# One core, two attentions: KH of group 0 in two equal loads, row maxima from tile 12, Q of the next unit asked for in the 9th step

## The chip, the core and the metric

The kernel runs on one core of a Trainium2 chip. The metric is the device time of one execution in microseconds; below 0.3% (some 2.8 us) two versions of this kernel cannot be told apart.

## The reference

Input x has 2048 rows of 448. Two attentions with 16 heads of 28 read it, and a gate per row mixes their outputs:

```python
g = sigmoid((x * gate_w).sum(-1, keepdims=True))
a = A_ref(x, A_wqkv, A_wo)   # each position attends to 8 positions back, 2 apart
b = B_ref(x, B_wqkv, B_wo)   # softmax(q k^T * Dh**-0.5) v over all 2048 positions
return g * a + (1 - g) * b
```

All is float32. A product of two float32 matrices is made of three products of "high" and "low" parts (a value rounded to fp32r, and the rest).

## The kernel before, in words

**Tile stage.** 92 tiles (`tiles`, indices 0 to 91; the loop at L451) project x. Tiles 0 to 27 give Q and K of B, 128 features by 512 positions each; tiles 28 to 43 give V of B; tiles 44 to 91 give q, k and v of A. The first 12 tiles are (position block, feature block) pairs from `tiles`: K of head group 0 comes from tiles 0, 3, 6 and 7, one block of 512 positions each. Tiles 0 to 9 (`FULL` = 10) use the whole TensorE array and four accumulators of two banks (`PS`) in turn. From tile 10 on the array is used in two halves of 64 rows (`project_halves`, L310): each half sums half of the products in its own bank of `PJ` = PS0 or PS1, and ScalarE copies both out (L348, L362). A Q or K tile has 21 such half matmuls.

**Row maxima (S1).** The softmax of B needs the row maxima before the scores. They come from a first score matrix that uses the high parts only. In 80 of the tiles, from `S1_START` on, four half-array score matmuls (`s1_half`, L155; L144) stand between the products, two into each pair of banks of `PM` = PS2 and PS3, and VectorE reduces each pair (L162). In the tile with index `S1_START` the two pairs stand later in the tile than in the others (L318). The first of these four tiles reads columns 0 to 511 of `KH[0]`, the next one columns 512 to 1023, and so on. The rest of the maxima are made in the main loop, three score matmuls a step (L1014, L148).

**SP's order.** All loads and stores of this stage go out on one queue, SP, in program order: for each of the tiles 0 to 9 two stores (`qk_store`, L331) of its high and low parts to DRAM, and between them the loads of weights, of Q for the maxima (`load_qhi`, L131) and of `KH[0]` back from DRAM (`load_k`, L104: four DMAs, one per head, of 28 rows each). A DMA that must wait holds back all that are behind it on SP.

**Main loop.** 16 units (head group, block of 512 queries) of 16 steps, `st` = 0 to 255 (L1052). A step multiplies 128 keys with the unit's Q (L1024), ScalarE takes the exponentials (L1027, two of 128 x 1024), TensorE sums them with V (L978), and VectorE reduces maxima. Work is hung on steps by hand ("pre" at the step's start, "dve", "end"). GpSimd (POOL) runs the local attention A, 8 chunks of 56 columns, in an order that a planner with fixed costs writes out, and between these pieces the parts of B's ending that are listed next. `load_q(u + 1)` (L119) asks for Q of the next unit: four DMAs of high parts, four of low parts, two of the negated maxima (10 in all), at the start of step 12 of unit u.

**Ending of a unit (L907 to L920).** During the unit that follows, counted in its steps: 1 copy the sums out (`osb`); 3 store the row sums; 6 VectorE inverts them, POOL multiplies them with the gate (`finv`, L847), SP stores the result (`rs<-finv`, L851); 8 SP loads it back, spread over partitions (`rbc`, four DMAs, L856); 12 POOL multiplies (`on`, L885); 15 ScalarE rounds the product (`onhi`, L889, ahead of that step's exponentials); then `onlo` on POOL and the stores. Loads of the low parts of K (`KL<-qk_lo`) for later groups hang on the end of steps 30, 72 and 136, and SP's loads of A's chunks (`qt`, `kt`, `vt`) go out at the start of a step, behind its "pre" work.

Of the kernel before, what the change touches and what calls it, by code (L numbers as in the profile page):

```python
# [15 lines left out]
S, D, H, DH = 2048, 448, 16, 28  # L16
# [4 lines left out]
NU = NG * NB  # L21
# [4 lines left out]
def gated_mix_kernel(ctx: ExitStack, tc: tile.TileContext, xT, xn, gw, wA, wB, woAB, out):  # L26
# [4 lines left out]
    qk_hi = dram.tile([2 * D, S], F32R, name="qk_hi")  # L31
# [41 lines left out]
    KH = [cp.tile([128, S], F32R, name=f"KH{i}") for i in range(2)]  # L73
# [26 lines left out]
    def dma_r(dst, src):  # L100
        nc.sync.dma_start(dst.bitcast(F32), src.bitcast(F32))  # L101


    def load_k(g, t, src, c=slice(0, S)):  # L104
        for h in range(4):
            r = D + 112 * g + DH * h
            dma_r(t[32 * h:32 * h + DH, c], src[r:r + DH, c])
# [98 lines left out]
    with tc.tile_pool(name="xp", bufs=1) as xp, tc.tile_pool(name="wp", bufs=2) as wp:  # L206
# [28 lines left out]
        def split_x(nb):  # L235
            r, t = xst[:, nb, 0:3, :], xst[:, nb, 3, :]
            for kt in range(3):
                split(xh[nb][:, kt, :], xl[nb][:, kt, :], r[:, kt, :])
            tail = xh[nb][:, 3, :]
            nc.scalar.activation(tail, t, AF.Copy)  # L240
            o = LOW[nb]
            nc.vector.tensor_tensor(out=tail[o], in0=t[o], in1=tail[o].bitcast(F32), op=ALU.subtract)
# [3 lines left out]
        def load_w(wi, tails=(False, True)):  # L246
            src, cols = WSRC[wi]
            if wi not in wraw:
                wraw[wi] = raw3(), wp.tile([128, 450], F32, tag="wt", name="wt"), sum(c1 - c0 for c0, c1 in cols) + 2 * (wi == GATE)
            r, t, _ = wraw[wi]  # L250
            for tail in tails:
                o = 0
                for c0, c1 in cols:
                    e = o + c1 - c0
                    if tail:
                        both(t[:, o:e], src[384:448, c0:c1])
                    else:
                        nc.sync.dma_start(r[:, :, o:e], src[0:384, c0:c1].rearrange("(k p) c -> p k c", p=128))
                    o = e

                if wi == GATE:
                    if tail:
                        both(t[:, o:o + 2], gw[0:2, 384:448].rearrange("i p -> p i"))
                    else:
                        for kt in range(3):
                            nc.sync.dma_start(r[:, kt, o:o + 2],
                                              gw[0:2, 128 * kt:128 * kt + 128].rearrange("i p -> p i"))

        def split_w(wi, kts):
            if wi not in wsets:  # L270
                wsets[wi] = [wp.tile([128, 4, 450], F32R, tag=g, name=f"{g}{wi}") for g in ("wh", "wl")]
            wh, wl = wsets[wi]
            r, t, n = wraw[wi]
            for kt in kts:
                split(wh[:, kt, :n], wl[:, kt, :n], r[:, kt, :n] if kt < 3 else t[:, :n], nc.gpsimd)
# [151 lines left out]
        def split_third():  # L427
            c = slice(256, 384)
            for kt in range(3):
                split(wh0[:, kt, c], wl0[:, kt, c], wr1[:, kt, 128:256])  # L430
            split(wh0[:, 3, c], wl0[:, 3, c], wt0[:, c])
# [9 lines left out]
        tiles.extend((4 + i, "a", i, j) for i in range(3) for j in js)  # L441


        FULL, S1_START = 10, 11

        parts = []

# [3 lines left out]
        for n, t in enumerate(tiles):  # L451
            wi = t[0]
            for w in loads:
                if loads[w] == n:
                    load_w(w)
            for w in splits:
                i, k = (n - splits[w][0]) * splits[w][1], splits[w][1]
                if 0 <= i < 4:
                    split_w(w, range(i, i + k))
            if n == 0:  # L460
                split_third()
            if n in (3, 5):
                split_x((n + 1) // 2)
            if n < FULL:
                project(n)
            else:
                project_halves(n, [S1_START <= m < S1_START + 80 for m in (n, n + 1)])
            if t[1] == "qk":
                qk_tile(n, t[2], t[3])
            elif t[1] == "v":  # L470
                add_halves(n, V[:, t[2], :, 0:DH])
            else:
                a_tile(n, t[2], t[3])
            if n == 0:
                split_x(1)
            while fini and fini[0][0] <= n:
                fini.pop(0)[1]()
            if n in (2, 3):
                load_w(1, (n == 3,))
            if n == 3:  # L480
                load_qhi(0)
            if n == 7:
                load_k(0, KH[0], qk_hi, slice(0, 1536))
            if n == 8:
                load_k(0, KH[0], qk_hi, slice(1536, S))
            if n == 16:
                for i in (1, 2):
                    nc.sync.dma_start(a_scr[i][:, 0:NJ, :].rearrange("c j e -> c (j e)").rearrange(
                        "c (a b) -> c a b", b=NJ), omg[0:8, None, :].to_broadcast([8, 56, NJ]))
            if n == 32:  # L490
                nc.gpsimd.memset(V[:, :, :, DH:], 1.0)
            if n == 22:
                load_k(1, KH[1], qk_hi)
            if n == 62:
                load_k(0, KL[0], qk_lo)
            if parts and parts[0][0] <= n:
                _, u, t = parts.pop(0)
                max_store(u, max_turn(t.bitcast(F32)))
            if finished and n < len(tiles) - 3:
                u = finished.pop(0)  # L500
                parts.append((n + 3, u, max_parts(u)))
            if n == 64:
                gate = []
                for sgn, dst in ((-1.0, g_t), (1.0, omg)):
                    e = sp.tile([128, NJ], F32, name="ez")
                    nc.scalar.activation(e, zt, AF.Exp, scale=sgn)
                    nc.gpsimd.tensor_tensor(out=e, in0=e, in1=V[:, 0, :, DH], op=ALU.add)
                    gate.append((dst, e))
            if n in (66, 68):
                nc.vector.reciprocal(*gate.pop(0))  # L510
            if n == 70:
                r = max_turn(omw)
                for a in range(4):
                    nc.sync.dma_start(og_scr.rearrange("(j p) -> j p", j=NJ)[:, 32 * a:32 * a + 32],
                                      r[32 * a:32 * a + NJ, :])
            if n == 76:
                load_q(0)
# [170 lines left out]
    for c in range(8):  # L688
# [20 lines left out]
        n = 0  # L709
# [342 lines left out]
    for u in range(NU):  # L1052
        g, b = divmod(u, NB)
        for kt in range(NJ):
            st = NJ * u + kt
            now[0] = st
            if kt == 12 and u + 1 < NU:
                load_q(u + 1)
            run("pre", st)
            issue("sp", st, 0)  # L1060
            if st >= A_START:
                issue("pool", st, 4.2)
            if not adone and not any(lists.values()) and st > stored[0]:
                a_done(st)
            cur = {}
            left = s1e - s1c[0]
            for a in scores(u, kt, cur):
                if a == 2:
                    run("mid", st)
            run("dve", st)  # L1070
            if u and kt == 6:
                late["dve"] += 0.25
            if finished:
                v = finished.pop(0)
                t = max_parts(v)
                late["dve"] += 0.3
                turned = {}
                lag = 2 if v < NU - 1 else 1
                at("dve", st + lag, lambda t=t, w=turned: w.update(r=max_turn(t.bitcast(F32))))
                at("end", st + lag, lambda v=v, w=turned: max_store(v, w["r"]))  # L1080
            issue("dve", st, DLIM)
            issue("act", st, 0)
            run("act", st)
            if prev is not None:
                do_av(prev)
            prev = (kt, cur, g)
            if OPS and st >= OPS[0]:
                op_some(st, 7)
            run("end", st)
            step = 2.25 if left else 2.1  # L1090
            late["dve"] = max(0.0, late["dve"] + 0.58 * min(3, left) - step)
            late["pool"] = max(0.0, late["pool"] - step)
            if st == OP0 + 31:
                op_load_b(2, 3)
            if not OPS and s1c[0] == s1e:
                s1_close()
                at("pre", st + 1, lambda: op_t(0))
                at("end", st + 1, lambda: op_split(0))
                OPS.append(st + 2)
# [61 lines left out]
```

## Time and profile before

| | |
|---|---|
| runs | 916.68, 918.61, 918.80 us; median 918.61 |
| profiled execution | 918.6 us, of which the instructions span 916.7 us |
| busy share: PE, VectorE, ScalarE, POOL | 99%, 80%, 71%, 68% |
| mean granted TensorE clock | 0.997 of full speed |
| tile stage, main loop | to about 258 us, from there to 887 us |

PE is TensorE; an instruction counts as busy while it is in the pipeline, so 99% says only that little time passes without any. The views used below: the list of waits (who waited for whom), the instructions of an engine in order of time, the chain of waits that ended last, and busy time by stretch.

### The profile page before, as it was taken

To read this page: it belongs to the slowest core of one execution; us is meant where nothing else is said; L and a number is where in the kernel's file an instruction comes from. 1 tells how busy PE (TensorE), PEld (TensorE's weight loads), DVE (VectorE), ACT (ScalarE), POOL (GpSimd) and SP (SyncE) were. 2 spreads that over 40 slices of the span, in tenths; PEclk is the share of its full clock that TensorE was granted. 3 is DMA by queue.
4 is the path that set the end of the run, shared out by engine and by line. 5 is a ranking of instruction groups with operands and counts; after the bars stand their busy time and mean duration, and the time that the engine had idled before them with its cause. 6 is when DMAs were issued, how large, how long until landed. Compare 5 with 4: busy or idle time off the path is not lost.

```text
span 916.7 us, 20680 instructions
## 1 busy us (share of the span) xinstructions
PE 904.7 (99%) x8396; PEld 539.3 (59%) x8396; DVE 731.4 (80%) x977; ACT 652.1 (71%) x802; POOL 620.9 (68%) x485
## 2 busy tenths in 40 slices
PE   9899999999999999999999999999999999999998
PEld 7688999999954444444444444443444444466667
DVE  6388999999979999999999999999999888400012
ACT  6356434343378898888888898988989889854551
POOL 2289856564469799999999999999994952300100
PEclk9999999999999999999999999999999999999999
DMA  9867603444372341335135232530412123553422
GB/s 268 275 203 220 177 11 83 132 122 120 103 249 70 97 126 44 86 112 127 44 96 153 86 102 55 144 79 23 115 42 53 34 66 102 145 162 112 131 90 93
DMA packets 101118, 104.29 MB, mean 114 GB/s; under 512 B 61652, under 2 KB 71252, under 8 KB 100240
## 3 DMA queue, kind: packets, MB, share of 16 engines
q1 hardware_dynamic: 100880, 102.72, 39.5%
q8 instruction: 65, 1.06, 0.5%
q10 hardware_dynamic: 144, 0.26, 0.1%
q14 instruction: 29, 0.24, 0.1%
HBM read 61.99 MB, written 40.48 MB: 112 GB/s over the span
## 4 chain that ended last, share of the span: by engine, by line
PE 80%; POOL 11%; DMA 3%; SPq 2%; ACT 2%; issue 1%; DVE 0%; POOLq 0%; ACTq 0%; DVEq 0%
PE T L1024 22%; PE av L978 20%; PE r L298 15%; PE T L817 8%; PE r L293 7%; PE r L144 4%; POOL prod L613 3%; POOL oat L668 3%; PE T L144 3%; POOL prod L663 2%; SPq L101 2%; ACT P L1027 1%; PE T L795 1%; DMA KL<-qk_lo 1%; DMA V<-in_xT 1%
## 5 line engine op out<-in xcount | busy, mean ns | idle before, releaser
L1027 ACT ACTIVATE P<-T 128x1024 f32<-128x1024 f32 x512 | 497.4, 1025 | 81.0 <-PE T L1024 79.6
L148 DVE TENSOR_REDUCE MX<-T 128x1 f32<-128x512 f32 x470 | 441.3, 954 | 33.6 <-PE T L144 19.6
L978 PE MATMUL av<-P,V 128*32 128x512 f32 x2048 | 272.7, 605 | 0.0
L1024 PEld LDWEIGHTS T<-QH,KH 30*128 30x128 f32 x1024 | 90.8, 181 | 222.4 <-ACT P L1027 199.9
L144 PE MATMUL T<-KH,QP 28*128 28x512 f32 x704 | 219.6, 454 | 0.1
L162 DVE TENSOR_REDUCE MX<-r 128x2 f32<-128x1024 f32 x160 | 192.5, 1221 | 28.3 <-PE r L144 23.6
L1024 PE MATMUL T<-QH,KH 30*128 30x512 f32 x1024 | 211.2, 489 | 3.0 <-ACT P L1027 2.0
L1024 PE MATMUL T<-QH,KL 28*128 28x512 f32 x1024 | 185.7, 395 | 0.0
L1024 PE MATMUL T<-QL,KH 28*128 28x512 f32 x1024 | 183.5, 392 | 0.0
L613 POOL TENSOR_TENSOR prod<-qt,kt 128x896 f32<-128x896 f32 x64 | 135.2, 2117 | 1.4 <-DMA kt<-a_scr 1.4
L362 ACT ACTIVATE raw<-r 128x896 f32<-128x896 f32 (+1 forms) x64 | 58.9, 921 | 96.7 <-PE r L298 96.7
L668 POOL TENSOR_TENSOR oat<-oat,prod 128x896 f32<-128x896 f32 x56 | 118.3, 2113 | 2.4
L144 PE MATMUL r<-KH,QP 64*128 64x512 f32 x320 | 98.9, 393 | 3.4 <-DMA KH<-qk_hi 3.4
L144 PEld LDWEIGHTS T<-KH,QP 28*128 28x128 f32 x704 | 86.0, 181 | 27.1 <-ACT P L1027 20.3
L663 POOL TENSOR_TENSOR prod<-vt,L 128x896 f32<-128x896 f32 x56 | 95.6, 1708 | 0.5
L363 POOL TENSOR_TENSOR ast<-raw 128x448 f32<-128x448 f32 x48 | 55.5, 1156 | 57.8 <-ACT raw L362 49.4
L1024 PEld LDWEIGHTS T<-QL,KH 28*128 28x128 f32 x1024 | 93.3, 184 | 0.0
L1024 PEld LDWEIGHTS T<-QH,KL 28*128 28x128 f32 x1024 | 91.8, 183 | 0.9
L298 PE MATMUL r<-wh,xh 64*128 64x448 f32 (+1 forms) x512 | 87.8, 363 | 0.0
L978 PEld LDWEIGHTS av<-P,V 128*32 128x32 f32 x2048 | 40.3, 108 | 77.2 <-issue 72.2
L805 DVE TENSOR_TENSOR oalo<-T,oah 128x384 fp32r<-128x384 f32 x16 | 8.9, 557 | 90.8 <-ACT onhi L804 87.7
L298 PE MATMUL r<-wh,xl 64*128 64x448 f32 (+1 forms) x384 | 70.9, 363 | 0.0
(110 smaller groups left out, 1157.0 us busy)
## 6 DMA issues: line engine op xcount, KB each, us to landing
a_scr<-ast SPq DMA_DIRECT2D x24, 448.0 KB
qk_hi<-qkh SPq DMA_DIRECT2D x24, 256.0 KB
qk_lo<-qkh SPq DMA_DIRECT2D x24, 256.0 KB
rbc<-rs SPq DMA_DIRECT2D x60, 64.0 KB
QP<-qk_hi SPq DMA_DIRECT2D x64, 56.0 KB
KL<-qk_lo SPq DMA_DIRECT2D x16, 224.0 KB
QH<-qk_hi SPq DMA_DIRECT2D x64, 56.0 KB
QL<-qk_lo SPq DMA_DIRECT2D x64, 56.0 KB
```

The lines of the kernel that those rows point to most:

```text
L144: nc.tensor.matmul(bank, qhis[u][h % 2][r, 128 * qs:128 * qs + 128], KH[u // NB % 3][r, 512 * kc:512 * kc + 512], start=True, stop=True)
L148: r = nc.vector.tensor_reduce(MX[:, n % NMX:n % NMX + k], bank, axis=X, op=ALU.max)
L162: nc.vector.tensor_reduce(m, PM[k], axis=X, op=ALU.max)
L293: nc.tensor.matmul(bank, ws[c][rows, k, t[4]:t[4] + 128], x, start=first, stop=last)
L298: nc.tensor.matmul(bank[:, 0:cols], x, ws[c][rows, k, 0:cols], start=first, stop=last)
L613: nc.gpsimd.tensor_tensor(out=p, in0=qt[c], in1=kvt["k", c % 2][:, HALO - DIL * w:HALO - DIL * w + NJ, :], op=ALU.mult)
L663: nc.gpsimd.tensor_tensor(out=dst.rearrange("p j (h d) -> p j h d", d=DH), in0=kvt["v", c % 2][:, HALO - DIL * w:HALO - DIL * w + NJ, :].r ...
L668: nc.gpsimd.tensor_tensor(out=oat[c], in0=oat[c], in1=oat[c, w], op=ALU.add)
L817: writes(bank, nc.tensor.matmul(bank[:, :D], src, wo[c][:, k, :], start=(first and k == ks[0] and i == 0), stop=(last and k == ks[-1] and ...
L978: nc.tensor.matmul(av[32 * h:32 * h + 32, :], V[:, kt, 4 * g + h, :], tiles_[h], start=(kt == 0), stop=(kt == NJ - 1), skip_group_check=True)
L1024: nc.tensor.matmul(bank[a], (KH[g % 3], KH[g % 3], KL[g % 2])[t][r, ks], (qh, ql, qh)[t][r, :], start=(t == 0), stop=(t == 2))
L1027: e = nc.scalar.activation(p, RP[0] if a == "2" else mine, AF.Exp, scale=SCALE).ins
```

## The change

Three edits. `KH[0]` was loaded as columns 0 to 1535 behind tile 7's stores and 1536 to 2047 behind tile 8's; now columns 0 to 1023 go out behind tile 6's stores and 1024 to 2047 behind tile 8's. The maxima start in tile 12 and end in tile 91 (tile 11 to 90 before). `load_q(u + 1)` stands at step 8 of units 0 to 11 and stays at step 12 in the later ones.

```diff
-        FULL, S1_START = 10, 11
+        FULL, S1_START = 10, 12
...
-            if n == 7:
-                load_k(0, KH[0], qk_hi, slice(0, 1536))
-            if n == 8:
-                load_k(0, KH[0], qk_hi, slice(1536, S))
+            if n in (6, 8):
+                load_k(0, KH[0], qk_hi, slice(512 * (n - 6), 512 * (n - 6) + 1024))
...
-            if kt == 12 and u + 1 < NU:
+            if kt == (8 if u < 12 else 12) and u + 1 < NU:
                 load_q(u + 1)
```

## Rows read from the trace of the kernel before

**Rows 1.** Page, part 4: share of the chain of waits by engine.
```profile
PE 80%; POOL 11%; DMA 3%; SPq 2%; ACT 2%; issue 1%; DVE 0%; POOLq 0%; ACTq 0%; DVEq 0%
```

**Rows 2.** Waits of PE, whole span: us in total, times, longest us.
```profile
PE r L144 <- DMA KH<-qk_hi: 3.4, 2, 2.2
...
PE T L1024 <- DMA QH<-nm: 0.7, 1, 0.7
```

**Rows 3.** ScalarE in time, 30 to 76 us: start, duration, instruction, [idle before].
```profile
36.23 1.03 ACT L348 ACTIVATE raw<-r 128x1024 f32<-128x1024 f32 x1 [2.14 <-PE r L293]
44.82 1.03 ACT L348 ACTIVATE raw<-r 128x1024 f32<-128x1024 f32 x1 [7.57 <-PE r L293]
...
50.65 1.03 ACT L348 ACTIVATE raw<-r 128x1024 f32<-128x1024 f32 x1 [1.47 <-PE r L144]
```

**Rows 4.** Busy time by stretch: length, PE/PEld/DVE/ACT/POOL (count), clock, DMA share, GB/s.
```profile
41.30:44.70 3.40, 3.24 (x16) 2.80 (x18) 1.96 (x2) 0.00 (x0) 0.00 (x0) 0.50 0.83 295
```

**Rows 5.** SP in time, 0 to 50 us: tile 7's store, KH's load.
```profile
32.96 0.59 SPq L101 DMA_DIRECT2D qk_hi<-qkh  x1
...
35.79 1.60 SPq L101 DMA_DIRECT2D KH<-qk_hi  x4
```

**Rows 6.** Chain of waits, 30 to 46 us: tile 6's store, KH.
```profile
31.58 4.15 DMA qk_hi<-qkh
...
37.01 4.32 DMA KH<-qk_hi
```

**Rows 7.** PE and VectorE in time, 246 to 270 us.
```profile
255.20 0.39 PE L144 MATMUL r<-KH,QP 64*128 64x512 f32 x1
...
258.17 0.49 PE L144 MATMUL T<-KH,QP 28*128 28x512 f32 x1
...
255.63 1.22 DVE L162 TENSOR_REDUCE MX<-r 128x2 f32<-128x1024 f32 x1 [0.23 <-PE r L144]
```

**Rows 8.** SP in time, 400 to 480 us (units 4, 5).
```profile
421.97 0.34 SPq L851 DMA_DIRECT2D rs<-finv  x1
422.41 1.64 SPq L101 DMA_DIRECT2D KL<-qk_lo  x4
424.14 1.70 SPq L856 DMA_DIRECT2D rbc<-rs  x4
...
460.73 0.42 SPq L602 DMA_DIRECT2D qt<-a_scr  x1
...
462.16 1.83 SPq L856 DMA_DIRECT2D rbc<-rs  x4
```

**Rows 9.** Chain of waits, 420 to 440 us: KL's fourth head.
```profile
423.67 6.16 DMA KL<-qk_lo
```

**Rows 10.** SP in time, 560 to 625 us (units 8, 9).
```profile
570.52 1.70 SPq L856 DMA_DIRECT2D rbc<-rs  x4
...
611.61 1.69 SPq L101 DMA_DIRECT2D QH<-qk_hi  x4
...
615.05 1.07 SPq L101 DMA_DIRECT2D QH<-nm  x2
```

**Rows 11.** POOL in order of time: `on` in units 4 and 8.
```profile
432.38 1.29 POOL L885 TENSOR_TENSOR on<-osb,rbc 128x512 f32<-128x512 f32 x1
...
580.14 1.29 POOL L885 TENSOR_TENSOR on<-osb,rbc 128x512 f32<-128x512 f32 x1
```

**Rows 12.** `on` in unit 5, its own view: duration, first and last start.
```profile
L885 POOL TENSOR_TENSOR on<-osb,rbc x1: 1288/1288/1288, 472.0 to 472.0; 128x512 f32<-128x512 f32 x1
```

**Rows 13.** ScalarE in order of time: `onhi` in units 4, 5 and 9.
```profile
437.14 0.63 ACT L889 ACTIVATE onhi<-on 128x512 fp32r<-128x512 f32 x1
...
473.89 0.63 ACT L889 ACTIVATE onhi<-on 128x512 fp32r<-128x512 f32 x1
...
619.58 0.63 ACT L889 ACTIVATE onhi<-on 128x512 fp32r<-128x512 f32 x1 [1.03 <-POOL on L885]
```

**Rows 14.** Waits of POOL, 309 to 700 us: total, times, longest.
```profile
POOL nmt L181 <- ACT nmv L180: 4.1, 1, 4.1
```

## The prediction

> **What bounds the kernel now.** I read the chain of waits first. PE carries 80% of it and POOL 11% [rows 1], so TensorE sets the time except in stretches where POOL does; PE's own list of waits says where something else enters. It has few: 3.4 us for `KH` at the first maxima and 0.7 us for the last part of a unit's Q [rows 2]. The edits touch both, and the list understates the one and overstates the other.
>
> The `KH` wait costs more than 3.4 us. ScalarE copies tile 10 out at 36.23 and tile 11 at 44.82 us; the two tiles that follow take 50.65 - 44.82 = 5.83 us, so 2.91 us each [rows 3]. Tile 11 took 8.59 us, 5.7 us too long. The rest is the clock: after the idle time the granted clock stands at 0.50 (1.2 in place of 2.4 GHz) for the 3.4 us from 41.30 on [rows 4], which costs half of that, 1.7 us.
>
> The 0.7 us for Q are worth nothing by themselves if POOL is late anyway. POOL waits once between 309 and 700 us, at its start, for ScalarE [rows 14]; from there it runs without a gap. Its product `on` feeds ScalarE's `onhi`, which stands ahead of a step's exponentials, and with them ahead of PE. In unit 9 `onhi` had to wait 1.03 us for it [rows 13]. So from 309 to 619 us the path is POOL's: whatever PE gains in between it loses again at 619 us, and each microsecond that POOL waits in there comes through. After that wait the margin in unit 9 is zero; in unit 5 it is 473.89 - (472.0 + 1.29) = 0.6 us [rows 12, 13].
>
> **Edit 1 and 2: the maxima start a tile later, `KH` in halves.** A Q or K tile has 21 half matmuls and 4 more with maxima: 2.91 / 25 = 0.117 us each. Tile 11 without them takes 21 x 0.117 = 2.45 us in place of 8.59: -6.1 us. Tile 91 gets them instead: 4 x 0.117 = +0.5 us. Sum -5.6 us, if no new wait comes. That depends on two landings.
>
> First half. Its stores (tiles 0 and 3) are long out. It takes the place of tile 7's store on SP, so it is issued from 32.96 on, four DMAs in some 1.6 us [rows 5], the last at about 34.2; with the 4.32 us that `KH`'s fourth head took [rows 6] it lands at 38.5. ScalarE's copy of tile 10 at 36.23 [rows 3] follows the tile's end by some tenths; I put the end at 35.8. Tile 11 then ends at 38.3, and in tile 12 twelve half matmuls stand ahead of the first maxima: needed at 39.7. Margin 1.2 us: cost 0 (bounds 0 and, if it waits half as long as before, 2.8 us).
>
> Second half. Tile 7's store is now issued 1.6 us later, at 34.6, and with 4.15 us [rows 6] is out at 38.8. Four more issues, the last at some 40.2; with 4.32 us it lands at 44.5. Tile 14 needs it at 38.3 + 2 x 2.91 + 4 x 0.117 = 44.6. That is on the edge. I take 0; bounds 0 and 2.8 us (1.1 us late and one stretch at half clock, 1.7 us).
>
> Tile 91's maxima end against the main loop. There the second reduction ended at 255.63 + 1.22 = 256.85, 1.65 us after the last score matmul of its tile (255.20) began [rows 7]. In tile 91 some six half matmuls, 0.7 us, follow that matmul; then comes the main loop, whose third instruction group writes `T1`, which I take to lie in the bank pair that is still being reduced. It waits about 0.9 us. Before, this step had waits of its own, shorter (its first maxima began with the loop, at 258.17 [rows 7], the next two behind ScalarE's copy of tile 91). I take +0.7 us; bounds 0 and 1.2. POOL is put off with PE: it waits for ScalarE at 309 us [rows 14].
>
> **Edit 3: Q asked for at step 8.** Q's ten DMAs occupy SP from 611.61 to 616.12, 4.5 us [rows 10]. Before, they came behind `rbc`, which POOL's `on` needs; now they come ahead of it, since `rbc` hangs on the end of step 8 and the loads on its start. Ahead of them stays `rs<-finv` of step 6, which SP holds until POOL has made `finv` [rows 8]. So `rbc` lands 4.5 us later wherever SP went from one to the other without a pause. Is there room? Where `rbc` goes out soon after `rs` with nothing large ahead of it, and `on` comes four steps later, I count on it. In three units a large load stands ahead of `rbc`, and there it is short:
> - Unit 4: SP issued `rs`, `KL`, `rbc` at 421.97, 422.41 and 424.14 [rows 8]. `KL` landed at 423.67 + 6.16 = 429.83 [rows 9] and `rbc`, behind it, before `on` began without a wait at 432.38 [rows 11]; I take 431.0. With 4.5 us it lands at 435.5: POOL waits 3.1 us (by the ends of the bracket, 1.9 to 4.5).
> - Unit 5: SP's `qt` and `kt` (460.73) stand between, `rbc` follows at 462.16 [rows 8]; with 6.2 us as `KL` had, 468.4. It moves by 4.5 and by POOL's 3.1, to 476.0; `on` would come at 472.0 + 3.1 = 475.1 [rows 12]: 0.9 to 1.0 more (bounds 0 and 4.5).
> - Unit 8: `rbc` at 570.52 behind `KL` [rows 10], so landed at 576.7; moved by 4.5 + 4.1 it is there at 585.3, `on` would come at 580.14 + 4.1 = 584.2 [rows 11]: 1.1 more (bounds 0 and 4.5).
>
> POOL loses 5.2 us by unit 9; I bound it by 0 and 7. PE follows: in unit 4 `onhi` still comes in time (435.5 + 1.3 = 436.8 against 437.14 [rows 13]), in unit 5 it waits some 4 us, and in unit 9 PE is 5.2 us later than without the edit. If PE's clock falls in that long wait, the 1.7 us come out of the 5.2, since POOL goes on. The 0.7 us of [rows 2] vanish as a wait and are part of what POOL then takes back. A's chunk loads are put off by 4.5 us as well; POOL never waited for one in this stretch [rows 14], and the code asks for each at least four steps, some 9 us, ahead of its use: 0.
>
> **Sum.** The profiled execution took 918.6 us (span 916.7 and 1.9 around it), the median of the runs. 918.6 - 5.6 + 0.7 + 5.2 = 918.9 us.
>
> **A rule against the middle of this sum.** Here `rbc`'s time depends on what SP sent before it: `KL`'s 224 KB took 6.16 us in such a row [rows 9]. The Trainium skill, "DMA: Bandwidth & Descriptors", section "Anatomy of one DMA — SWDGE (gpsimd) path", puts a DMA of the other issuing path at a fixed 2.0 us plus its bytes over 436 GB/s. By that an estimate for `KL` is 2.5 us and for one `rbc` 2.2 us; `rbc` would be there before `on` in all three units, POOL would wait for nothing, and the time would be that of the first rival below. The trace does not agree: 6.16 us.
>
> **The rivals.**
> - `rbc` is in time, POOL loses under 2.5 us. For it: the landing of `rbc` has no row of its own, only brackets, and with the early ends of all three (1.9 + 0 + 0) POOL loses 1.9. With none lost: 918.6 - 5.6 + 0.7 = 913.7 us. Against it: `KL`'s landing is a row, and it moves with the 4.5 us.
> - The second half of `KH` is the new wait (slower than before). Its place is tile 14, its point of decision a landing after 44.6 us. 1.1 us late with one stretch at half clock adds 2.8: 921.7 us. For it: no margin, and DMA is 0.83 busy there [rows 4]. Against it: 4.32 us is the landing behind stores that filled the queue, and a short wait need not bring the clock down.
> - The change doesn't do what it says: the first half still waits (for tile 7's store, or behind the queue), tile 12 stalls as tile 11 did, half as long: 918.9 + 2.8 = 921.7 or a bit more.
>
> **How the numbers follow.** Less than 0.3%, 2.8 us, cannot be told from no change. Chances: my forecast 0.50 (915.8 to 921.4); `rbc` in time 0.34 (913 to 915.8); second half late 0.11; first half late 0.05. So faster 0.34, same 0.50, slower 0.16. The range reaches to the first rival's price and the others': 913.3 to 921.7, with a tenth left out at either end. The likeliest's own range is 916 to 921.
>
> **What would show it.** Tile 11's copy near 38.7 us, no wait of PE for `KH`, the granted clock at full between 30 and 50 us: edit 1 right; a wait at about 44 to 45 us, the second rival. The first step of the main loop with PE waiting for VectorE's L162: the 0.7 us. POOL's list of waits with `on` behind `rbc`, in units 4, 5 and 8, in sum 5 us, and `onhi` behind `on` for about as long: edit 3's price. If `on` has no such wait, the sum is wrong by 5 us; if PE's first waits for `KH` are still there, by 6.

## The result and the profile after

| | before | after |
|---|---|---|
| median of 9 runs each | 918.80 us (916.01 to 922.98) | 923.05 us (920.40 to 925.72) |
| ratio of the two, 95% interval | | 1.0047 [1.0027, 1.0068] |
| profiled execution | 918.6 us, span 916.7 | 920.4 us, span 918.4 |
| main loop (from where ScalarE begins to wait for the first step to the end of the last step's first exponential) | 258.28 to 887.36 | 252.80 to 889.23 |
| mean granted clock, profiled | 0.997 | 0.998 |

The changed kernel is slower by about half a per cent, and the time lies above the forecast range. A second measurement of the same kernel gave 1.0021 [1.0009, 1.0033] (e9 below). The steps say where it went: the main loop starts 5.5 us earlier and takes 636.4 us in place of 629.1, 7.3 us more. What follows it is 0.1 us shorter. In the rows below the numbers of lines behind L480 or so are two lower than before.

**The tile stage.** ScalarE in time, as in [rows 3]; the second of the two copies ends tile 11:

```profile
36.31 1.03 ACT L348 ACTIVATE raw<-r 128x1024 f32<-128x1024 f32 x1 [2.14 <-PE r L293]
38.85 1.03 ACT L348 ACTIVATE raw<-r 128x1024 f32<-128x1024 f32 x1 [1.51 <-PE r L293]
```

It was at 44.82 before. PE's waits over the whole span, as in [rows 2] (us in total, times, longest), have no row for `KH` or for Q; VectorE's reductions have come in their place, and the first row, ScalarE's exponentials, has grown:

```profile
PE T L1022 <- ACT P L1025: 5.0, 6, 1.6
...
PE T L144 <- DVE MX L148: 1.1, 1, 1.1
PE T L1022 <- DVE MX L148: 0.6, 1, 0.6
...
PE T L144 <- DVE MX L162: 0.3, 1, 0.3
```

The last row is the turn from the tile stage to the main loop ([rows 7]), here in PE's order of time:

```profile
253.46 0.50 PE L144 MATMUL T<-KH,QP 28*128 28x512 f32 x1 [0.27 <-DVE MX L162]
```

**POOL.** Its waits between 290 and 740 us, as in [rows 14], have one more row, and the product `on` in units 4, 5 and 8 ([rows 11, 12]) shows it:

```profile
POOL on L883 <- DMA rbc<-rs: 7.1, 3, 4.2
POOL nmt L181 <- ACT nmv L180: 4.1, 1, 4.1
```

```profile
431.37 1.29 POOL L883 TENSOR_TENSOR on<-osb,rbc 128x512 f32<-128x512 f32 x1 [4.21 <-DMA rbc<-rs]
...
472.03 1.29 POOL L883 TENSOR_TENSOR on<-osb,rbc 128x512 f32<-128x512 f32 x1 [0.99 <-DMA rbc<-rs]
...
581.99 1.29 POOL L883 TENSOR_TENSOR on<-osb,rbc 128x512 f32<-128x512 f32 x1 [1.85 <-DMA rbc<-rs]
```

SP's order in unit 4 ([rows 8]) has Q's ten DMAs, of which the four to `QH` are shown, between `rs` and `KL`; the chain of waits then gives the landing of `rbc` a row, 6.49 us from the start of its last issue ([rows 9] was `KL`'s):

```profile
416.70 0.34 SPq L849 DMA_DIRECT2D rs<-finv  x1
417.15 1.64 SPq L101 DMA_DIRECT2D QH<-qk_hi  x4
...
421.60 1.74 SPq L101 DMA_DIRECT2D KL<-qk_lo  x4
423.39 1.75 SPq L854 DMA_DIRECT2D rbc<-rs  x4
```

```profile
424.72 6.49 DMA rbc<-rs
```

**How PE got to know.** `onhi` on ScalarE, as in [rows 13], waits for `on` in units 4, 5, 8 and 9, but for little each time:

```profile
432.69 0.63 ACT L887 ACTIVATE onhi<-on 128x512 fp32r<-128x512 f32 x1 [0.67 <-POOL on L883]
...
473.35 0.63 ACT L887 ACTIVATE onhi<-on 128x512 fp32r<-128x512 f32 x1 [0.59 <-POOL on L883]
...
583.31 0.63 ACT L887 ACTIVATE onhi<-on 128x512 fp32r<-128x512 f32 x1 [1.18 <-POOL on L883]
...
621.43 0.63 ACT L887 ACTIVATE onhi<-on 128x512 fp32r<-128x512 f32 x1 [1.51 <-POOL on L883]
```

The largest loss comes another way. ScalarE makes `nmv` of unit 5 at 448.62; POOL, which is behind, gets to its part `nmt` at 454.98; VectorE's transpose `nms`, which stands in VectorE's queue ahead of the next reductions, has stood idle 2.47 us for it. ScalarE, POOL and VectorE in order of time:

```profile
448.62 0.22 ACT L180 ACTIVATE nmv<-m 128x16 f32<-128x16 f32 x1
...
454.98 0.22 POOL L181 TENSOR_TENSOR nmt<-nmv,nmt 128x16 fp32r<-128x16 f32 x1
...
455.23 0.21 DVE L186 STREAM_TRANSPOSE nms<-nmt 128x32 f32<-128x32 f32 x1 [2.47 <-POOL nmt L181]
```

PE then waits 1.1 and 0.6 us for the reductions, and the granted clock falls. Busy time by stretch (columns as in [rows 4]); the first row, the tile stage from 30 us on, has no such fall:

```profile
30.00:50.00 20.00, 20.00 (x158) 17.50 (x157) 9.91 (x10) 9.23 (x13) 13.89 (x13) 1.00 0.91 291
...
455.00:458.40 3.40, 1.62 (x17) 0.69 (x15) 3.17 (x7) 0.73 (x2) 3.40 (x5) 1.00 0.02 2
458.40:461.80 3.40, 3.40 (x25) 1.37 (x23) 2.32 (x4) 1.59 (x2) 3.32 (x3) 0.50 0.22 48
461.80:465.00 3.20, 3.20 (x38) 1.10 (x31) 2.83 (x6) 2.86 (x3) 3.20 (x2) 1.00 0.34 101
```

PE was busy for 1.62 of 3.40 us, and in the 3.4 us after that it had 1.2 in place of 2.4 GHz, which costs half of them, 1.7 us. In sum the two steps of this place took 4.61 and 3.90 us; in a kernel without the wait (the third experiment) they took 2.31 and 2.12: +4.1 us.

### The profile page after: what moved, and what is told of

Same layout as the page of the kernel before. It is cut to its first block, busy times and chain, and to the rows that moved or that the text cites. A ratio compares the mean times of both kernels' runs of the same rounds, so it can differ in the third digit from the quotient of the medians.

```text
span 918.4 us, 20670 instructions
## 1 busy us (share of the span) xinstructions
PE 905.2 (99%) x8396; PEld 541.2 (59%) x8396; DVE 731.7 (80%) x977; ACT 652.5 (71%) x802; POOL 620.8 (68%) x485
## 4 chain that ended last, share of the span: by engine, by line
PE 76%; POOL 12%; SPq 4%; DMA 4%; ACT 2%; DVE 1%; issue 1%; POOLq 0%; ACTq 0%; DVEq 0%
PE T L1022 20%; PE av L976 18%; PE r L298 14%; PE T L815 8%; PE r L293 7%; PE r L144 5%; POOL prod L611 3%; POOL oat L666 3%; POOL prod L661 3%; SPq L101 2%; PE T L144 2%; DMA rbc<-rs 2%; ACT P L1025 1%; SPq L854 1%; DVE MX L148 1%
## 5 line engine op out<-in xcount | busy, mean ns | idle before, releaser
L1025 ACT ACTIVATE P<-T 128x1024 f32<-128x1024 f32 x512 | 497.2, 1024 | 85.2 <-PE T L1022 83.6
L144 PE MATMUL r<-KH,QP 64*128 64x512 f32 x320 | 86.7, 390 | 0.0
L298 PE MATMUL r<-wh,xh 64*128 64x448 f32 (+1 forms) x512 | 85.4, 362 | 0.0
```

Source lines behind the costliest of these rows:

```text
L144: nc.tensor.matmul(bank, qhis[u][h % 2][r, 128 * qs:128 * qs + 128], KH[u // NB % 3][r, 512 * kc:512 * kc + 512], start=True, stop=True)
L298: nc.tensor.matmul(bank[:, 0:cols], x, ws[c][rows, k, 0:cols], start=first, stop=last)
L1025: e = nc.scalar.activation(p, RP[0] if a == "2" else mine, AF.Exp, scale=SCALE).ins
```

## The experiments

Each was measured beside the kernel before on the same chip; the ratio is to that.

| label | what | median us (range, runs) | before | ratio [95%] |
|---|---|---|---|---|
| e1_first_two_edits | edits 1 and 2 | 913.67 (912.90 to 914.57, 4) | 919.49 | 0.9937 [0.9913, 0.9960] |
| e2_third_edit | edit 3 | 925.86 (924.48 to 930.62, 6) | 919.49 | 1.0078 [1.0048, 1.0109] |
| e3_q_behind_rbc | all, Q behind `rbc` | 913.36 (913.17 to 913.88, 4) | 919.49 | 0.9934 [0.9911, 0.9957] |
| e4_kl_later | all, `KL` 5 steps later | 916.25 (914.72 to 918.35, 10) | 919.49 | 0.9962 [0.9947, 0.9977] |
| e5_q_behind_nmt_vector | e3, `nmt` on VectorE | 919.47 (918.74 to 920.29, 10) | 919.30 | 1.0001 [0.9989, 1.0013] |
| e6_kh_halves_alone | edit 1 | 915.90 (915.03 to 918.85, 10) | 919.30 | 0.9972 [0.9960, 0.9985] |
| e7_s1_later_alone | edit 2 | 916.12 (913.52 to 916.47, 6) | 919.30 | 0.9959 [0.9944, 0.9974] |
| e8_all_nmt_vector | all, `nmt` on VectorE | 925.41 (922.64 to 926.70, 4) | 919.30 | 1.0062 [1.0039, 1.0084] |
| e9_changed_again | all three edits | 921.76 (919.59 to 923.43, 12) | 919.73 | 1.0021 [1.0009, 1.0033] |
| e10_nmt5_later | e3, unit 5's `nmt` later | 914.43 (913.50 to 915.77, 6) | 919.73 | 0.9944 [0.9922, 0.9966] |
| e11_turn_later | all, transposes later | 920.35 (919.14 to 922.52, 12) | 919.73 | 1.0002 [0.9989, 1.0016] |
| e12_onhi9_later | e3, unit 9's `onhi` later | 914.75 (913.35 to 915.11, 6) | 919.28 | 0.9950 [0.9934, 0.9965] |

### Which edit costs

**e1_first_two_edits.** The changed kernel with Q at step 12 again.

```diff
-            if kt == (8 if u < 12 else 12) and u + 1 < NU:
+            if kt == 12 and u + 1 < NU:
```

> Only the two edits of the tile stage (KH in two equal loads, maxima from tile 12); Q stays at step 12. Theory 1 (the Q loads put rbc off, POOL waits for it, and POOL is the path from 309 to 620 us): the main loop begins 5.2 to 5.5 us earlier, POOL waits 0 us for rbc, time 5 us under before, about 913.5. Rival (the tile stage's gain is not kept, POOL or a later wait takes it back without the third edit too): within 1.5 us of before.

Its waits for Q and of `onhi` (1.03 us in [rows 13]) remain, and POOL has none for `rbc`. PE's waits and ScalarE's (total, times, longest):

```profile
PE T L1022 <- DMA QH<-nm: 0.4, 1, 0.4
...
ACT onhi L887 <- POOL on L883: 1.3, 1, 1.3
```

So the first two edits are worth 5.8 us by themselves, and all that is lost is lost by the third.

**e2_third_edit.** The kernel before with Q at step 8 alone.

```diff
-            if kt == 12 and u + 1 < NU:
+            if kt == (8 if u < 12 else 12) and u + 1 < NU:
```

> Only Q at step 8; the tile stage as before. Theory 1: POOL waits some 7 us for rbc in units 4, 5 and 8 (4.2, 1.0, 1.9 in the changed kernel), and the time is 7 to 10 us over before, 926 to 929. Rival (the third edit is near free, and the first two cost): POOL's waits do not come through, within 2 us of before.

It costs 6.4 us, with no edit to the tile stage. In its profile the tile stage takes 1.8 us longer than before all the same (PE waits 3.9 us for `KH` in place of 3.4, and the clock stays at half for 6.8 us in place of 3.4); the main loop takes 5.9 us longer (634.98 against 629.08), as much as POOL waits. The waits of POOL, ScalarE and VectorE are those of the changed kernel, the transpose's too:

```profile
POOL on L885 <- DMA rbc<-rs: 5.9, 3, 3.1
...
ACT onhi L889 <- POOL on L885: 3.2, 3, 1.5
...
DVE nms L186 <- POOL nmt L181: 2.4, 2, 2.1
```

**e3_q_behind_rbc.** All three edits, but Q is asked for at the end of step 8, behind `rbc`, not at its start.

```diff
+    for u in range(12):
+        at("end", NJ * u + 8, lambda u=u: load_q(u + 1))
...
-            if kt == (8 if u < 12 else 12) and u + 1 < NU:
+            if kt == 12 and u >= 12 and u + 1 < NU:
```

> All three edits, but in units 0 to 11 Q is asked for at the end of step 8, behind rbc, in place of the start: the same loads, one step's SP order turned round. Theory 1: POOL waits 0 us for rbc, no wait of VectorE for POOL's nmt, time as with the first two edits, 913 to 914. Rival (earlier Q traffic as such, or what it does to A's chunk loads, is the cost): as the changed kernel, 921 to 924.

SP in unit 4 sends the same DMAs in the other order, `rbc` 4.6 us earlier than in the changed kernel:

```profile
416.63 0.34 SPq L849 DMA_DIRECT2D rs<-finv  x1
417.07 1.64 SPq L101 DMA_DIRECT2D KL<-qk_lo  x4
418.81 1.70 SPq L854 DMA_DIRECT2D rbc<-rs  x4
420.69 3.81 SPq L101 DMA_DIRECT2D QH<-qk_hi  x4
```

POOL waits for no `rbc`, VectorE for no `nmt`, PE for no Q, and `onhi` waits 1.3 us in unit 9, as in e1. The main loop takes 252.79 to 881.84, 629.05 us, what it took before. The order of two pieces of work on one queue makes the whole difference: 9.7 us between this median and that of the changed kernel, 8.4 against its second measurement (neither beside it in the same comparison). And the wait for Q was worth nothing: e1 has it, this kernel does not, and they differ by 0.3 us with ranges that overlap. This is the fastest of the versions tried.

**e4_kl_later.** The changed kernel with the low parts of K asked for five steps later, so that they don't stand ahead of `rbc` in units 4 and 8.

```diff
-    ... (72, 2, KL[0], qk_lo), ... (136, 3, KL[1], qk_lo)
+    ... (77, 2, KL[0], qk_lo), ... (141, 3, KL[1], qk_lo)
```

> All three edits, and the KL loads of steps 72 and 136 moved to the ends of steps 77 and 141, so that rbc has Q's ten DMAs ahead of it but not KL. Theory 1 with the queue (rbc's landing is what stands ahead of it on SP): POOL's waits in units 4 and 8 (4.2 and 1.9 us) go to 0, unit 5's 1.0 stays or falls, time 6 us under the changed kernel, about 915 to 916. Rival (the 4.5 us of SP issue alone make rbc late): waits of 2 us or more stay in both units, 920 or more.

Of POOL's three waits for `rbc` one is left, that of unit 5:

```profile
POOL on L883 <- DMA rbc<-rs: 1.8, 1, 1.8
```

So in units 4 and 8 it takes both, Q's 4.5 us and `KL` ahead of `rbc`; Q alone fits into the four steps. In unit 5, where SP sends three loads of A's chunks ahead of `rbc`, it does not. Beside this wait the profile shows two falls of the clock (0.66 over 255 to 260 and over 474 to 479 us), which e3's does not. The main loop is 3.5 us longer than e3's (632.55 against 629.05): 1.6 us are in unit 0, with the first fall; the other 1.9 are about POOL's wait of 1.8, and the second fall lies within them.

### The two halves of the first gain

**e6_kh_halves_alone** and **e7_s1_later_alone.** Edit 1 alone, and edit 2 alone.

```diff
e6, against e1:                     e7, against before:
-        FULL, S1_START = 10, 12    -        FULL, S1_START = 10, 11
+        FULL, S1_START = 10, 11    +        FULL, S1_START = 10, 12
```

> Only KH in two equal loads; maxima from tile 11 and Q at step 12 as before. Theory 1: the first half lands at 38.1 us, tile 11 needs it at about 37.3, so PE waits 0.8 us, the clock stays up, and tile 91 has no maxima to wait for: 4.5 to 5 us under before, 914 to 915. Rival (the late first tile is what brings the gain): PE waits 2 us or more, the clock falls, 917 or more.

> Only the maxima from tile 12 on; KH loaded as 1536 and 512 columns, Q at step 12. Theory 1: KH's fourth head lands at 41.3 us, tile 12 needs it at 39.7, PE waits 1.6 us; of the 5.6 us some 3 to 4 stay, and 0.5 go at tile 91: 915 to 917. Rival (the halves bring the gain): two waits and a fall of the clock as before, 918 or more.

Each leaves a short wait of PE for `KH`, the first row from e6 and the second from e7:

```profile
PE r L144 <- DMA KH<-qk_hi: 1.1, 2, 0.9
```

```profile
PE r L144 <- DMA KH<-qk_hi: 1.0, 1, 1.0
```

After neither does the granted clock fall there. The edits are worth 3.4 and 3.2 us alone and 5.8 together: both take from the same wait, and only together they take all of it. e7's profile (916.47 us, near its median) holds one thing more: at the start of the main loop the clock falls for 3.4 us, and unit 0 takes 38.95 us in place of 37.42 in e1, whose clock does not fall there.

### Is it the transpose's wait, or POOL's loss?

**e9_changed_again.** The changed kernel, nothing edited, beside e10 and e11.

> The changed kernel again, for another profiled execution and a time beside the next two. Theory 1: POOL again waits some 7 us for rbc in three places; the profiled execution that took 920.4 us had one fall of the clock in the main loop, one of the median's length (923) has two or more, each worth 1.7 us. Rival (the 2.6 us are elsewhere): the same waits and one fall in an execution of 922 to 924.

The three waits for `rbc` and that of the transpose come again, POOL's a little smaller:

```profile
POOL on L883 <- DMA rbc<-rs: 6.5, 3, 3.8
...
DVE nms L186 <- POOL nmt L181: 2.5, 1, 2.5
```

PE waits 1.2 and 0.6 us behind the transpose as before, but here the clock does not fall. It falls 18 us later, behind a wait of `onhi` of 2.12 us in unit 5. Busy time by stretch:

```profile
455.00:458.40 3.40, 1.99 (x21) 0.83 (x21) 3.40 (x7) 0.93 (x2) 3.40 (x3) 1.00 0.04 4
458.40:461.80 3.40, 3.40 (x42) 1.52 (x34) 3.40 (x7) 2.95 (x4) 3.32 (x3) 1.00 0.24 71
...
476.04:479.45 3.41, 3.41 (x23) 1.19 (x15) 2.43 (x4) 2.18 (x4) 3.33 (x4) 0.50 0.01 2
```

The loss reaches PE at other places than in the first profile, and the sum is the same: the main loop is 6.7 us longer than e3's (635.71 against 629.05), and POOL waited 6.5 us for `rbc`.

**e11_turn_later.** The changed kernel with all transposes but the last four steps behind in place of two, so that VectorE need not wait for POOL.

```diff
-                lag = 2 if v < NU - 1 else 1
+                lag = 4 if v < NU - 1 else 1
```

> The changed kernel with VectorE's transpose of nmt (and its store) four steps behind the maxima in place of two, so that a late POOL does not hold VectorE up. Theory 1 in its strict form (PE must lose what POOL loses, by onhi if not by VectorE): POOL's waits for rbc stay at 7 us, the profiled time stays within 1 us of 920.4, and only falls of the clock can differ: 920 to 923. Rival (VectorE's wait for nmt and the fall of the clock behind it add to POOL's loss): 3 us or more under the changed kernel.

The transpose waits no more, and `onhi` does instead, in unit 5 and unit 9 (ScalarE in time):

```profile
472.76 0.63 ACT L887 ACTIVATE onhi<-on 128x512 fp32r<-128x512 f32 x1 [3.63 <-POOL on L883]
...
620.56 0.63 ACT L887 ACTIVATE onhi<-on 128x512 fp32r<-128x512 f32 x1 [1.86 <-POOL on L883]
```

This is the course that the prediction had written down ("in unit 5 it waits some 4 us"), and it comes to the same: 920.35 against 921.76 us, 1.4 less, ranges overlapping. (The profile puts POOL's longest wait, 3.9 us in unit 4, down to an exponential, which `on` does not read; in the other profiles the wait in this place is for `rbc`, and it is taken for that here, which is not shown.) POOL's waits before `on` are 5.8 us, and by unit 10 PE is 6.0 us behind e3. Which engine hands POOL's loss on to PE hardly matters up to there; POOL's loss does. Then the main loop loses 1.4 us more: behind the wait of `onhi` in unit 9 the clock falls a second time:

```profile
622.95:626.36 3.41, 3.41 (x24) 1.10 (x24) 2.02 (x3) 2.51 (x4) 3.33 (x3) 0.50 0.02 5
```

There `onhi` has waited for POOL for the last time, and no later wait takes this loss in.

**e8_all_nmt_vector** and **e5_q_behind_nmt_vector.** `nmt` computed by VectorE ahead of its transpose, in the changed kernel and in e3: meant to take POOL out of this path.

```diff
-        nc.gpsimd.tensor_tensor(out=t[:, 16:32], in0=v, in1=t[:, 0:16].bitcast(F32), op=ALU.subtract)
-        return t
+        return t, v
...
+    def max_low(tv):
+        t, v = tv
+        nc.vector.tensor_tensor(out=t[:, 16:32], in0=v, in1=t[:, 0:16].bitcast(F32), op=ALU.subtract)
+        return t.bitcast(F32)
...
-                at("dve", st + lag, lambda t=t, w=turned: w.update(r=max_turn(t.bitcast(F32))))
+                at("dve", st + lag, lambda t=t, w=turned: w.update(r=max_turn(max_low(t))))
```

> The changed kernel with nmt's subtraction on VectorE. Theory 1: VectorE no longer waits 2.5 us for POOL in unit 5, so the two steps of 4.6 and 3.9 us and the fall of the clock there go; POOL is some 4 us further ahead when it comes to rbc, so it waits longer for rbc but PE loses less: 3 to 4 us under the changed kernel, 919 to 920. Rival (PE must lose POOL's 7 us one way or the other): the same time as the changed kernel, onhi waits in place of nms.

> As e3 (all three edits, Q behind rbc at the end of step 8), and the small subtraction that makes nmt stands on VectorE, right ahead of the transpose that reads it, in place of POOL. Theory 1 (POOL is the path from its 4.1 us wait for ScalarE's nmv to onhi of unit 9): that wait of POOL goes, POOL runs some 4 us further ahead, onhi's 1.3 us wait in unit 9 goes with it, 1.3 us under e3, about 912. Rival (VectorE, 96% busy, is as much the path): its 16 more instructions cost what POOL gives, 913.4 or more.

Both failed as experiments on POOL: with the subtraction on VectorE, VectorE is held up by POOL in another way. The view of `nmt` in e5 gives the least, middle and longest of its 16 subtractions in ns; POOL took 0.22 us for one. Below it, POOL and VectorE in time:

```profile
L185 DVE TENSOR_TENSOR nmt<-nmv,nmt x16: 165/232/2584, 94.6 to 791.4; 128x16 fp32r<-128x16 f32 x16
```

```profile
648.84 2.11 POOL L615 TENSOR_TENSOR prod<-qt,kt 128x896 f32<-128x896 f32 x1
...
649.85 1.13 DVE L185 TENSOR_TENSOR nmt<-nmv,nmt 128x16 fp32r<-128x16 f32 x1
```

VectorE's instruction ends at 650.98, POOL's at 650.95. It is so each time that it meets a TENSOR_TENSOR of POOL, 18 times in e5 and e8: it ends 0.02 to 0.04 us after one of POOL's. The other 14 took 0.16 to 0.18 us. e5 lost 6.1 us against e3. Its main loop starts 2.8 us later than e3's: the subtraction at 94.56 lasted 2.58 us, and PE waited 1.6 us behind it (second row below); it also waited 0.6 us in sum for `KH`. The loop takes 2.9 us more, with four waits of PE for VectorE (first row), and the steps with the subtractions of 0.99, 0.58, 0.80 and 1.13 us are 1.05, 0.61, 0.84 and 0.93 us longer than e3's:

```profile
PE T L1029 <- DVE MX L148: 2.3, 4, 0.6
PE r L144 <- DVE MX L162: 1.6, 1, 1.6
```

The wait of `onhi` in unit 9 is gone in e5, which shows only that PE came later to it.

### What holds the best version

**e10_nmt5_later** and **e12_onhi9_later.** Both start from e3, which keeps the 1.3 us of `onhi` in unit 9. The first lets POOL make unit 5's `nmt` two steps later (POOL's wait of 4.1 us, [rows 14], lies in front of it); the second asks for unit 9's `onhi` a step later.

```diff
e10:
+        def low():
+            nc.gpsimd.tensor_tensor(out=t[:, 16:32], in0=v, in1=t[:, 0:16].bitcast(F32), op=ALU.subtract)
+        if u == 5:
+            at("end", now[0] + 2, low)
...
-                lag = 2 if v < NU - 1 else 1
+                lag = 4 if v == 5 else 2 if v < NU - 1 else 1
e12:
+             8: (1, 3, 6, 8, 12, 16, 17, 19)}.get(
```

> As e3 (all three edits, Q behind rbc), and only for unit 5, whose maxima are the first that end inside the main loop, POOL's nmt two steps later in its order and its transpose and store two steps later as well. Theory 1: POOL no longer stands 4.1 us at 303 us, is 4 us further ahead up to unit 9, onhi's 1.3 us wait there goes: 1.3 us under e3, 911.5 to 912.5. Rival (POOL was not the path; something else takes the place): as e3, 913 to 914.

> As e3 (all three edits, Q behind rbc), and in unit 9 alone onhi stands at the next step 0 in place of step 15, onlo one step later. Theory 1 (POOL reaches PE through onhi of unit 9, and what PE gains before is lost there): the wait of 1.3 us goes, POOL has the 2.3 us of a step more, the time falls by 1.3 us under e3, about 912. Rival (another wait for POOL takes its place at once): the same time, 913.4, and a wait elsewhere in units 9 or 10.

Neither gained (0.9944 and 0.9950 beside 0.9934, intervals overlapping). In e10 POOL's wait of 4.1 us is gone from its list. In its place POOL waits longer for VectorE: one wait of 2.7 us for `finv` (at 305.3 us) and one of 1.0 us for `lr` (at 328.2 us), which e3 has not; e3 has only the 11.6 us of the first row's 14.3. `onhi` in unit 9 waits as in e3:

```profile
POOL finv L851 <- DVE finv L850: 14.3, 2, 11.7
...
POOL lr L655 <- DVE lr L651: 1.0, 1, 1.0
...
614.16 0.63 ACT L893 ACTIVATE onhi<-on 128x512 fp32r<-128x512 f32 x1 [1.28 <-POOL on L889]
```

In e12 that wait is gone from unit 9, and the next two units have it:

```profile
649.96 0.63 ACT L887 ACTIVATE onhi<-on 128x512 fp32r<-128x512 f32 x1 [0.28 <-POOL on L883]
686.76 0.63 ACT L887 ACTIVATE onhi<-on 128x512 fp32r<-128x512 f32 x1 [0.65 <-POOL on L883]
```

So the path that is left runs over POOL, and in e10 over VectorE ahead of it; these two changes, each at one place, only moved the wait.

## Why the prediction was wrong

**The tile stage was right.** Tile 11's copy was put at 38.7 us and came at 38.85; PE waits for no `KH`, and the clock stays at full. The main loop starts 5.5 us earlier, with 5.6 forecast. The second rival (second half late) and the third (first half still waits) fell by that; e6 and e7 show that both edits were needed for it. Tile 91's maxima cost 0.25 us in unit 0 (37.38 against 37.14 us from the loop's start to the first exponential of unit 1), not 0.7: the wait came, but 0.27 us long, not 0.9.

**The mechanism of edit 3 was right.** Q's loads ahead of `rbc` make POOL wait in exactly the three units named, and by unit 9 PE has lost what POOL lost: 7.3 us of main loop, of which 0.25 are unit 0's, against POOL's 4.21 + 0.99 + 1.85 = 7.05. e2 shows it by itself (5.9 and 5.9 us) and e3 takes it back. That the 0.7 us of [rows 2] are worth nothing was right too (e1 against e3). The rival of an `rbc` in time fell. The rule of the Trainium skill ("DMA: Bandwidth & Descriptors", section "Anatomy of one DMA — SWDGE (gpsimd) path") that was weighed against the sum is stated for a single DMA issued by GpSimd, and for one `rbc` it gave an estimate of 2.2 us. The trace does not agree for `rbc` on SP's queue: behind `KL` it has 6.49.

**Two steps failed, both in size.** The sum said 918.9 us, the median is 923.05: 4.15 us more. POOL's loss was put 1.85 us too small, and 2.65 us lie between the median and the profiled execution, which the sum had taken for the same. The 0.45 us too much for tile 91 and 0.1 us at the loop's start make up the rest.

**The first is the size of POOL's loss: 5.2 us in the sum, 7.05 measured.** Of its three terms unit 5 came out as forecast (1.0 and 0.99). Unit 4 was put at 3.1 and took 4.21: `rbc`'s landing before had been taken as 431.0, inside its bracket. With `rs` 5.27 us earlier now (421.97 to 416.70) and the landing at 424.72 + 6.49 = 431.21, and if `rbc` takes as long from its issue as before, it follows as 431.21 + 5.27 - 4.5 = 432.0, a few tenths ahead of the use at 432.38. The bracket's late end, 4.5, was the nearer one. Unit 8 was put at 1.1 and took 1.85, in the main for the same reason: the landing before had been taken as 576.7, and in the same way it follows as 577.2 (now 576.38 + 5.37 = 581.75, less 4.5, with `rs` at the same time as before). With the measured sizes the sum is 918.6 - 5.5 + 0.25 + 7.05 = 920.4 us, and the profiled execution took 920.4. That lies within the forecast range; what lifts the median above it is the second step.

**The path from POOL to PE was only half seen.** The prediction let `onhi` in unit 4 come in time and wait 4 us in unit 5. It waited 0.67 in unit 4, as the larger loss there makes it (432.66 for the end of `on`, against 437.14 - 5.27 = 431.87), and 0.59 in unit 5, for in between the transpose of unit 5's maxima had already passed the loss on. The trace of before had its margin. There the tile `nmt` and its reader in their own view (duration, first and last start):

```profile
L181 POOL TENSOR_TENSOR nmt<-nmv,nmt x1: 238/238/238, 456.0 to 456.0; 128x16 fp32r<-128x16 f32 x1
L186 DVE STREAM_TRANSPOSE nms<-nmt x1: 202/202/202, 457.7 to 457.7; 128x32 f32<-128x32 f32 x1
```

VectorE came to it 457.7 - 456.24 = 1.5 us after POOL was done; POOL 4.2 us late makes 2.7 us of wait, and 2.47 were measured. The error was to follow only one of POOL's results to PE. It cost nothing in the sum, as POOL's own loss sets it, and the clock's 1.7 us came out of that loss as the prediction said. e9, where the clock falls at another place, bears this out (6.7 us of main loop, 6.5 of POOL's waits).

**The second is that the sum stood on the profiled execution as the median, and why that failed stays open.** Before, the two were the same (918.6 and 918.61 us). After the change the profiled one is the shortest of its 9 runs, and again of 12 in the second measurement (919.59 with a median of 921.76), so the median is 2.2 and 2.65 us above what the profile explains. The sum has no term for that. Lower mean clocks go with longer times in part (six of the 9 runs show 0.995 or 0.996 and take 922.6 to 925.7 us), and one stretch of 3.4 us at half clock is 0.002 of the mean; but at 0.998 there are 920.4 and 923.2 us as well. No run of the changed kernel with a longer time was profiled, so whether these have more falls of the clock or longer waits for `rbc` was not settled. Other profiles show two places for a fall whose cost stays and that the changed kernel's two profiles lack: the start of the main loop (e4 and e7, 1.6 and 1.5 us) and behind the wait of `onhi` in unit 9 (e11, 1.4 us). e1 and e3, without the waits, scatter by 1.7 and 0.7 us, the changed kernel by 5.3 and 3.8.

## What to carry to other kernels

Before a load is moved forward on a queue, list what it passes, and take from the trace how much earlier than its use each of these lands; here the load gained 0.7 us that nobody needed and cost the transfer that it passed 4.5. Where a landing is known only by a bracket, and its late end touches the use, put the late end into the sum. Where waits are short and the clock may or may not fall behind them, one profiled execution need not be the median: leave room for falls that it does not have. And follow every result of an engine that will be late to its readers, not only the one that waited before: each reader in another engine's queue has its own margin.

## What the runs showed of the hardware

- How long `rbc` (four DMAs of 64 KB) took to land hung on what SP had sent just before it. From the start of its last issue it took 6.49 us in unit 4 and 5.37 in unit 8, behind four loads of 224 KB, and 4.80 us in unit 5 behind three chunk loads of 392 to 448 KB. In unit 4 of e4, where only Q's ten DMAs went ahead, `on` began without a wait for it 4.1 us after that issue.
- The four `QH` DMAs took SP 1.64 us in the changed kernel and 3.81 us in e3, where `KL` and `rbc` went ahead of them. The issues themselves were no longer (0.31 us each in e3); between them SP waited 2.7 us in sum, in four waits, for loads of `KL` to land.
- Waits of PE of 1.1 and 0.6 us, which left it busy for 1.62 of 3.40 us, were followed by 3.4 us at 0.50 of the clock, 1.7 us lost at that place. The same waits in e9 (1.2 and 0.6 us, busy for 1.99 of 3.40) were followed by none, nor were those of 0.9 and 1.0 us for `KH` in e6 and e7 (1.00 over 40 to 50 us in both).
- A subtraction of two 128x16 tiles on VectorE took 0.16 to 0.18 us with no TENSOR_TENSOR of POOL beside it, and up to 2.62 us with one: in 18 of 18 such cases it ended 0.02 to 0.04 us after one of POOL's (e5 and e8).
